# Dummy matmuls, transpose order and a copy's engine in the start-up of a two-layer SSM and GeGLU kernel

## The chip, the cores and the metric

The kernel runs on one core of a Trainium2 chip. The metric is the device time of one execution in microseconds (us).

## What is computed

Two layers, each a state-space block with a long convolution (A) followed by a gated feed-forward block (B), with shared weights, on 2048 rows of 576 features. The long convolution goes through a Fourier transform in the reference.

```python
def _A_ref(q, k, v, shift_k, ssm_k, ssm_D):
    ...                                   # k_shift: causal taps of k with shift_k (4 of them)
    kv = k_shift * v
    ...                                   # y = causal convolution of kv with ssm_k over 2048 rows
    y = y + kv * ssm_D[None, None, :]
    return q * y

def _B_ref(x, w_gate, w_up, w_down):
    return (_gelu(x @ w_gate) * (x @ w_up)) @ w_down

x = A_q
x = x + _A_ref(_layernorm(x, axis=-1), A_k, A_v, A_shift_k, A_ssm_k, A_ssm_D)
x = x + _B_ref(_layernorm(x, axis=-1), B_w_gate, B_w_up, B_w_down)
x = x + _A_ref(_layernorm(x, axis=-1), A_k, A_v, A_shift_k, A_ssm_k, A_ssm_D)
x = x + _B_ref(_layernorm(x, axis=-1), B_w_gate, B_w_up, B_w_down)
```

The features are 576, the feed-forward width 4608, the rows 2048; everything that comes in or goes out is bf16.

## The kernel before

The rows are cut into four blocks of 512, and each block into four row tiles of 128 (row `4p + i` of a block lies on partition `p`). The convolution is done block by block with a transform of 512 points written as matmuls: forward transform of the filter block and of `kv`, products on VectorE, inverse transform on TensorE. Block 0 needs only filter block 0, block 1 needs blocks 0 and 1, and so on.

The program has two stages.

**The start-up** (to about 45 us) does the convolution of block 0, the gate and the layernorm behind it, and the first gate and up matmuls. Its instructions are not written in a fixed order: `add(engine, cost, run, deps, ...)` enters a task with an estimated cost, and `Plan.order` simulates the engines with these costs. For each engine it takes, among the tasks that could start within 0.25 us of the earliest, the one with the highest rank plus priority (`prio`), where the rank is the longest chain of costs behind the task. A task that needs one of four PSUM banks (`bank=True`) gets one that is free, and a bank is free once the tasks in `frees` are over. The engines then run their instructions in this order, each waiting for its data.

In order of time the start-up holds, with the lines that matter here:

- dummy matmuls of `ones` by `ones` into bank 3 (L1139), 20 of them;
- four taps (L1197): a matmul broadcasts a row of `shift_k` over the partitions, ScalarE copies it (L1201). The last tap has dummy matmuls of its own behind it (`spare`, L1190);
- the shifted products: VectorE multiplies `k` by a tap (L1217), TensorE sums over the taps with identity matrices (L1226), VectorE multiplies by `v` (L1237);
- filter block 0 is transposed on TensorE (L1255, `turned_h0`), two groups of ten transposes. The 576 features are four pieces of 128 rows and one of 64. ScalarE copies each group (L1257), and VectorE adds `ssm_D` to one row (L1302);
- the forward transforms (L281 and L275), ScalarE's copies (L1293, L1319), VectorE's products (L316 to L320) and sums (L1347);
- the inverse transform for the four row tiles (L1361), each into a bank of its own;
- filter block 1 is transposed (L1275, `turned_h1`) into columns of these banks that the inverse leaves unused; VectorE copies the result, a small piece (L1277) and a large one (L1280), for each of two groups;
- dummy matmuls (`busy`, L1380), eight tasks of four, with priority -100;
- for each row tile: ScalarE's factor (L1408), VectorE's gate (L1417), ScalarE's square (L1436), GpSimd's root (L1445 and L1446), VectorE's norm (L1453), TensorE's transposes (L1467, and L1465 for a pair that is 64 columns wide), and a copy to `xnT`, on VectorE for row tiles 0 and 1 (L1472) and on ScalarE for 2 and 3 (L1475). The order of the tiles is 2, 0, 3, 1. ScalarE also keeps `y` for layer 1 (`keep`, L1428);
- the first halves of the first two gate and up blocks (`half_of`, L1008 with 256 columns), which need only row tiles 0 and 2. The second halves follow in the loop and need 1 and 3.

**The feed-forward loop** goes over units (layer, block) in three phases of the weights each. For each of 12 columns of a phase it does gate and up (L1008, TensorE), gelu (ScalarE) and a product (VectorE), then the down matmuls (L1601). Between these it fits in the convolution of the next blocks (L290, L301 and L343 on TensorE, products on VectorE). What goes in where is decided while the program is built, by a running estimate of the engines' times (`Pace`: `t.pe`, `t.dve`, `t.act`), which starts from what the start-up's plan leaves over. While block 1 is being made (`hurry`), a gelu takes one of two branches: with `t.act <= t.pe + 0.2` ScalarE copies the up half too and VectorE multiplies two bf16 tiles (L1572 to L1574); else VectorE multiplies straight out of PSUM (L1582, L1583).

Of the kernel before, what the change touches and what calls it, by code (L numbers as in the profile page):

```python
# [10 lines left out]
ACT = mybir.ActivationFunctionType  # L11
# [6 lines left out]
P = 128  # L18
# [4 lines left out]
HW = 288  # L23
# [48 lines left out]
class Plan:  # L72
# [8 lines left out]
    def add(self, eng, cost, run=None, deps=(), lat=0.0, bank=False, frees=(), ready=0.0, prio=0.0):  # L81
        task = Task(eng, cost, run, [d for d in deps if d is not None], lat, bank, list(frees), ready, prio)
        for b in task.frees:
            b.users += 1
        self.tasks.append(task)
        return task
# [607 lines left out]
def ssm_geglu_kernel(ctx, tc, A_q, A_k, A_v, A_shift_k, A_ssm_k, A_ssm_D, B_x, B_w_gate, B_w_up,  # L694
                     B_w_down, out):
    nc = tc.nc
    q2 = A_q[0]
    out2 = out[0]
    S, D = q2.shape
# [9 lines left out]
    NKC = D // HK  # L709
# [19 lines left out]
    def bank(n, name, shape=(P, 2, 512), dt=F32):  # L729
        return banks[n].tile(list(shape), dt, tag="pr", name=name)  # L730
# [358 lines left out]
    with tc.manual_schedule():  # L1089
# [3 lines left out]
        ND = D // P + 1  # L1093
        plan = Plan(4)
        add = plan.add
        with ExitStack() as es:
# [17 lines left out]
            for grid in (ident, below):  # L1114
                nc.gpsimd.memset(grid[:], 0.0)
            nc.sync.dma_start(out=sk1[SK:SK + 1, :, :].rearrange("p d j -> p (d j)"),
                              in_=A_shift_k.rearrange("d j -> (d j)").unsqueeze(0))
# [17 lines left out]
            warm = tmp.tile([P, 1], F32, name="warm")  # L1135
            nc.scalar.activation(out=warm[:], in_=conv.pis[:], func=ACT.Sin)
            ps = bank(3, "ps")
            for _ in range(20):
                nc.tensor.matmul(ps[:, 0, 0:P], lhsT=ones[:], rhs=ones[:], start=True, stop=True)  # L1139

            held = {}
# [1 line left out]
            def psum(key, task, shape=(P, 2, 512), dt=F32):  # L1143
                held[key] = bank(task.slot, "ps", shape, dt)
                return held[key]

            def chain(tasks):
                for a, b in zip(tasks, tasks[1:]):
                    b.deps.append(a)

            def later(make):

                box = []
                box.append(make(lambda f: (lambda: f(box[0]))))
                return box[0]
# [4 lines left out]
                out=jT[:, i, :, :], in0=colT[:], scalar=rowT[:, i:i + 1], in1=offs[:], op0=ALU.mult, op1=ALU.add), prio=50.0)  # L1160
# [25 lines left out]
            vneg = add("ACT", 0.9, vnegs, [vsin], prio=-20.0)  # L1186

            def spare(ps):
                for _ in range(2):
                    nc.tensor.matmul(ps[:, 1, 3 * P:4 * P], lhsT=ones[:], rhs=ones[:], start=True, stop=True)  # L1190


# [15 lines left out]
            for i0 in range(0, RT, 2):  # L1208
                accs = {i0: [], i0 + 1: []}
                first = {}  # L1210
                for j in range(conv.KS - 1, -1, -1):
# [9 lines left out]
                    for i in (i0, i0 + 1):  # L1221
# [7 lines left out]
                        a = later(lambda me: add("PE", 0.25, me(acc), [mults[-1]], bank=(j == conv.KS - 1), prio=20.0))  # L1229
# [5 lines left out]
                for i in (i0, i0 + 1):  # L1235
                    chain(accs[i])
                    kv0[i] = add("DVE", 0.74, lambda i=i: nc.vector.tensor_tensor(  # L1237
                        out=conv.halves(conv.vt_[0][:, i, :]), in0=held.pop(("kv", i))[:, :, 0:HW],
# [4 lines left out]
            hT, pairs1 = {}, []  # L1243
            hT0 = hp.tile([P, RT, D], BF16, tag="h", name="h")

            def turned_h0():
                outs = []
                hT[0] = lambda i: hT0[:, i, :]
                for g in range(RT // 2):
                    def fill_ps(task, g=g):  # L1250
                        pt = psum(("h", g), task, (P, 2, 1024), BF16)
                        for i in range(2):
                            for db in range(ND):
                                w = min(P, D - db * P)
                                nc.tensor.transpose(pt[:, i, db * P:db * P + w], hn[0][0:w, db, 2 * g + i:BS:RT], ident[0:w, 0:w])  # L1255
                    a = later(lambda me: add("PE", 1.05, me(fill_ps), bank=True, ready=HN_AT, prio=30.0))
                    outs.append(add("ACT", 1.12, lambda g=g: nc.scalar.copy(out=hT0[:, 2 * g:2 * g + 2, :], in_=held.pop(("h", g))[:, :, 0:D]),  # L1257
                                    [a], lat=0.1, frees=[a], prio=30.0))
                return outs

            def turned_h1(dep):


                W = D - P
                beside = lambda j: held["y", j].bitcast(BF16)
                hT[1] = conv.ht[1] = lambda i: pairs1[i // 2][:, i % 2, :]
                for g, j in ((0, 3), (1, 1)):
                    def fill_ps(g=g, j=j):
                        pairs1.append(conv.hrp.tile([P, 2, D], BF16, tag="hr", name="ht"))
                        for i in range(2):  # L1270
                            for db in range(ND):
                                w = min(P, D - db * P)
                                out = beside(j)[:, i, 2 * HW + (db - 1) * P:2 * HW + (db - 1) * P + w] if db else \
                                    beside(0)[:, g, 2 * HW + i * P:2 * HW + (i + 1) * P]
                                nc.tensor.transpose(out, hn[1][0:w, db, 2 * g + i:BS:RT], ident[0:w, 0:w])  # L1275
                    a = add("PE", 1.0, fill_ps, dep + [opened[0], opened[j], facs[j]], prio=-30.0)
                    add("DVE", 0.2, lambda g=g: nc.vector.tensor_copy(  # L1277
                        out=pairs1[g][:, :, 0:P], in_=beside(0)[:, g, 2 * HW:2 * HW + 2 * P].rearrange("p (i d) -> p i d", i=2)),
                        [a], frees=[opened[0]], prio=-10.0)
                    add("DVE", 0.6, lambda g=g, j=j: nc.vector.tensor_copy(  # L1280
                        out=pairs1[g][:, :, P:D], in_=beside(j)[:, :, 2 * HW:2 * HW + W]), [a], frees=[opened[j]], prio=-20.0 if g else -30.0)

            h0 = {}

# [24 lines left out]
            for m in KTS:  # L1309
                K0[m] = []  # L1310
                for s in range(2):
                    def fill_ps(task, m=m, s=s):
                        if s == 0:
# [3 lines left out]
                    a = later(lambda me: add("PE", 0.99, me(fill_ps), list(kv0.values()) + [tneg if m else tsin], bank=True,  # L1317
                                           prio=-4.0 * KTS.index(m)))
                    K0[m].append(add("ACT", 0.65, lambda m=m, s=s: nc.scalar.copy(  # L1319
                        out=kc[m][:, :, s * HW:(s + 1) * HW] if m == KTS[-1] else conv.halves(kc[m][:, s, :]),  # L1320
                        in_=held.pop(("k", m, s))[:, :, 0:HW]), [a], lat=0.1, frees=[a]))
# [34 lines left out]
            inv, opened = {}, {}  # L1356
# [6 lines left out]
            for i in (0, 2, 1, 3):  # L1363
# [5 lines left out]
                for kt, hs in ((0, (0, 1)), (1, (0, 1)), (3, (0,)), (3, (1,))):  # L1369
# [3 lines left out]
                                                      prio={(1, 0): -40.0, (0, 3): 10.0}.get((i, kt + hs[0]), 4.0 if i == 2 else 0.0))))  # L1373
# [4 lines left out]
            def busy():  # L1378
                for _ in range(4):
                    nc.tensor.matmul(held["y", 0][:, 1, 416:512], lhsT=ident[:], rhs=ident[:, 0:96], start=True, stop=True)  # L1380
            chain([add("PE", 0.22, busy, [inv[1], inv[3], opened[0]], frees=[opened[0]], prio=-100.0) for _ in range(8)])


            g0 = gvars[0]
# [19 lines left out]
            for j in (0, 2, 1, 3):  # L1404
# [33 lines left out]
                near = 10.0 if j in (0, 2) else 0.0  # L1438
                sq = add("ACT", 0.77, square, [gp], lat=0.05, prio=near if j else 0.0)

                def root(j=j):
# [2 lines left out]
                    ve = small.tile([P, 1], F32, tag="ve", name="ve")  # L1444
                    nc.gpsimd.tensor_scalar(out=ve[:], in0=v["ss"][:], scalar1=1.0 / D, scalar2=EPS, op0=ALU.mult, op1=ALU.add)  # L1445
                    nc.gpsimd.tensor_tensor(out=v["rstd"][:], in0=ve[:], in1=neghalf_t[:, 0:1], op=ALU.pow)  # L1446
                rt = add("POOL", 1.07, root, [sq], prio=near)

                def norm(j=j):
                    v = vs0[j]  # L1450
# [6 lines left out]
                def turn_xn(task, j=j):  # L1457
                    if 0 not in xnT_of:
                        xnT_of[0] = xtp.tile([P, NKC, CH], BF16, tag="xnT", name="xnT")
                    pt = psum(("xt", j), task, (P, 2, 1024), BF16)  # L1460
                    for b in range(NKC):
                        c0 = b * P if b < 5 else HK + (b - 5) * P
                        if b == 4:
                            for r0, c0 in ((0, 4 * P), (HK, 0)):
                                nc.tensor.transpose(pt[r0:r0 + HK, 0, 4 * P:5 * P], held["xn", j][:, c0:c0 + HK], ident[:])  # L1465
                            continue
                        nc.tensor.transpose(pt[:, b // 8, (b % 8) * P:(b % 8 + 1) * P], held["xn", j][:, c0:c0 + P], ident[:])  # L1467
                tx = later(lambda me: add("PE", 0.73, me(turn_xn), [no], bank=True))
                tok = slice(j * P, (j + 1) * P)
                view = lambda j=j: held["xt", j][:].rearrange("p a b -> p (a b)")[:, 0:NKC * P].rearrange("p (b q) -> p b q", q=P)  # L1470
                if j < 2:
                    c = add("DVE", 0.76, lambda tok=tok, view=view: nc.vector.tensor_copy(out=xnT_of[0][:, :, tok], in_=view()),  # L1472
                            [tx], frees=[tx])
                else:
                    c = add("ACT", 1.03, lambda tok=tok, view=view: nc.scalar.copy(out=xnT_of[0][:, :, tok], in_=view()),  # L1475
                            [tx], lat=0.1, frees=[tx])
                early_xn.append([c])


            turned_h1([loads[1]])  # L1480
            conv.nhr = 6
            conv.hr_free[0] = conv.hr_free[1] = NEVER
# [39 lines left out]
        for at, (wb, ph, ui, first, final) in enumerate(visits):  # L1522
# [33 lines left out]
            for fi in range(FP):  # L1556
                n, gi = divmod(wb * FP + fi, FG)
                w = wgu[n]
# [141 lines left out]
```

## Time and profile before

| | |
|---|---|
| three timed runs | 925.32, 927.99, 927.9 us; median 927.9 |
| profiled execution | 925.07 us, span 923.3 us |
| TensorE busy | 914.4 us (99%), 8101 matmuls |
| VectorE, ScalarE, GpSimd busy | 580.2, 326.0, 146.1 us |
| start-up, to 46.06 us: TensorE, VectorE, ScalarE busy | 44.31, 37.37, 33.10 us |
| largest group | L1008, gate and up, 5148 matmuls, 561.1 us |

The profile is of one execution. Times of the timeline count from the start of the span. A group's line gives the line of the code, the engine, the tile and what it is made from, and the shapes; what stands in brackets is the idle time of the engine just before and who ended it. A matmul's length includes its way through the array, so matmuls that follow each other overlap, and the distance of their starts tells the rate. The chain of waits is followed back from the last instruction to the first.

### The profile page before, as it was taken

To read this page: it belongs to the slowest core of one execution; us is meant where nothing else is said; L and a number is where in the kernel's file an instruction comes from. 1 tells how busy PE (TensorE), PEld (TensorE's weight loads), DVE (VectorE), ACT (ScalarE), POOL (GpSimd) and SP (SyncE) were. 2 spreads that over 40 slices of the span, in tenths; PEclk is the share of its full clock that TensorE was granted. 3 is DMA by queue.
4 is the path that set the end of the run, shared out by engine and by line. 5 is a ranking of instruction groups with operands and counts; after the bars stand their busy time and mean duration, and the time that the engine had idled before them with its cause. 6 is when DMAs were issued, how large, how long until landed. Compare 5 with 4: busy or idle time off the path is not lost.

```text
span 923.3 us, 19170 instructions
## 1 busy us (share of the span) xinstructions
PE 914.4 (99%) x8101; PEld 528.7 (57%) x8101; DVE 580.2 (63%) x1106; ACT 326.0 (35%) x594; POOL 146.1 (16%) x314
## 2 busy tenths in 40 slices
PE   9999999999999999999999999999999999999998
PEld 7746556565564665655645646546546556556555
DVE  8785885777898898768888874552333334432332
ACT  7674435533215145252123233451221224321211
POOL 5323102312114013230112101220000002100000
PEclk9999999999999999999999999999999999999999
DMA  9999996429617801992943820790820820787620
GB/s 239 278 265 257 241 251 115 127 67 252 190 48 177 229 1 28 250 250 48 254 137 94 162 67 29 131 190 13 155 78 1 152 81 14 138 209 169 140 65 27
DMA packets 125307, 129.69 MB, mean 140 GB/s; under 512 B 39714, under 2 KB 117411, under 8 KB 125220
## 3 DMA queue, kind: packets, MB, share of 16 engines
q1 hardware_dynamic: 116018, 92.92, 47.3%
q0 software_dynamic: 9056, 34.95, 11.6%
q8 instruction: 63, 1.03, 0.5%
q10 hardware_dynamic: 146, 0.59, 0.2%
q14 instruction: 24, 0.20, 0.1%
HBM read 108.09 MB, written 11.80 MB: 130 GB/s over the span
## 4 chain that ended last, share of the span: by engine, by line
PE 94%; DVE 3%; DMA 1%; ACT 0%; issue 0%; POOL 0%; SPq 0%; ACTq 0%; DVEq 0%
PE gu L1008 61%; PE dn L1601 28%; PE ps L281 1%; PE cps L290 1%; PE cps L343 1%; DMA hn<-in_A_ssm_k_dram 1%; DVE kc L602 1%; PE cps L301 0%; PE ps L1008 0%; PE ps L1226 0%; DVE ab L308 0%; DVE x_c L1417 0%; DVE cd L308 0%; ACT eo L303 0%; DMA xnT<-xn 0%
## 5 line engine op out<-in xcount | busy, mean ns | idle before, releaser
L1008 PE MATMUL gu<-xnT,wgu 64*128 64x512 bf16 x5148 | 561.1, 376 | 2.3 <-DVE x_c L1643 1.5
L1008 PEld LDWEIGHTS <-wgu 64*128 64x128 bf16 x5220 | 255.0, 94 | 304.6 <-issue 9.9
L1582 ACT ACTIVATE ga<-gu 128x512 f32<-128x512 f32 x256 | 152.8, 597 | 471.4 <-PE gu L1008 465.2
L1583 DVE TENSOR_TENSOR hT<-ga,gu 128x512 bf16<-128x512 f32 x256 | 175.6, 686 | 204.8 <-ACT ga L1582 203.3
L1601 PE MATMUL dn<-wd,hT 128*128 128x288 bf16 x2304 | 294.1, 286 | 0.0
L1601 PEld LDWEIGHTS <-hT 128*128 128x128 bf16 x2304 | 223.5, 98 | 65.3 <-issue 9.3
L840 POOL TENSOR_SCALAR means<-s 128x1 f32<-128x1 f32 x28 | 12.7, 453 | 236.7 <-DVE x_c L1637 205.3
L1645 DVE TENSOR_TENSOR x_c<-x_c,dn 128x576 f32<-128x576 f32 x32 | 24.1, 753 | 30.9 <-PE dn L1601 30.8
L1643 DVE SCALAR_TENSOR_TENSOR x_c<-dn,means,x_c 128x576 f32<-128x576 f32 x28 | 22.7, 815 | 26.8 <-PE dn L1601 26.7
L856 POOL TENSOR_TENSOR rstd<-ve,neghalf_t 128x1 f32<-128x1 f32 x56 | 35.2, 628 | 4.7
L320 DVE TENSOR_TENSOR prod<-prod 128x576 bf16<-128x576 bf16 x72 | 33.0, 458 | 2.5
L1572 ACT ACTIVATE ga<-gu 128x512 bf16<-128x512 f32 x30 | 17.9, 597 | 44.0 <-PE gu L1008 43.0
L303 ACT ACTIVATE eo<-cps 128x576 f32<-128x576 f32 x32 | 20.4, 650 | 25.0 <-DVE ab L308 9.8
L418 POOL DMA_DIRECT2D kr<-Kd x24 | 13.3, 553 | 87.2 <-DVE prod L319 86.0
L1624 DVE TENSOR_TENSOR xn<-x_c,dn 128x576 bf16<-128x576 f32 x15 | 11.3, 753 | 23.9 <-PE dn L1601 23.9
L422 POOL DMA_DIRECT2D hr<-Hd x36 | 19.5, 543 | 40.9 <-DVE prod L319 38.7
L1574 DVE TENSOR_TENSOR hT<-ga 128x512 bf16<-128x512 bf16 x31 | 13.1, 421 | 20.4 <-ACT ga L1573 20.4
L602 DVE TENSOR_TENSOR kc<-ab,cd 128x288 bf16<-128x288 f32 x64 | 25.6, 451 | 0.0
L840 POOL TENSOR_SCALAR nm<-s 128x1 f32<-128x1 f32 x28 | 8.7, 312 | 99.8 <-DVE x_c L892 99.8
L848 ACT ACTIVATE junk<-x_c,nm 128x576 bf16<-128x576 f32 x28 | 21.5, 767 | 4.9 <-POOL nm L840 4.9
L882 ACT ACTIVATE yh<-y,rstd 128x576 f32<-128x576 bf16 x28 | 21.4, 768 | 2.3 <-POOL rstd L856 2.3
L855 POOL TENSOR_SCALAR ve<-ss 128x1 f32<-128x1 f32 x56 | 15.2, 271 | 43.3 <-ACT junk L848 43.2
(180 smaller groups left out, 612.1 us busy)
## 6 DMA issues: line engine op xcount, KB each, us to landing
wgu<-in_B_w_gate_dram SPq DMA_DIRECT2D x45, 576.0 KB, 6.1
wd<-in_B_w_down_dram SPq DMA_DIRECT2D x30, 864.0 KB, 8.0
wgu<-in_B_w_up_dram SPq DMA_DIRECT2D x45, 512.0 KB, 8.3
hr<-Hd POOLq DMA_DIRECT2D x36, 288.0 KB, 7.3
kr<-Kd POOLq DMA_DIRECT2D x24, 288.0 KB, 5.9
Kd<-kc POOLq DMA_DIRECT2D x12, 288.0 KB, 6.7
k<-in_A_k_dram POOLq DMA_DIRECT2D x3, 1008.0 KB, 11.2
wgu<-in_B_w_up_dram SPq DMA_DIRECT2D x45, 64.0 KB, 8.4
```

The source lines that it names most:

```text
L320: nc.vector.tensor_tensor(out=dst[:, cols], in0=pr[:, 0, cols], in1=pr[:, 1, cols], op=ALU.subtract if part == 0 else ALU.add)
L602: nc.vector.tensor_tensor(out=into[k][:, plane, cols], in0=a, in1=b, op=op)
L840: nc.gpsimd.tensor_scalar(out=v["nm"][:], in0=v["s"][:], scalar1=-1.0 / D, scalar2=None, op0=ALU.mult)
L848: nc.scalar.activation(out=junk[:], in_=get_x(), func=ACT.Square, bias=v["nm"][:, 0:1], accum_out=v["ss"][:])
L856: nc.gpsimd.tensor_tensor(out=v["rstd"][:], in0=ve[:], in1=neghalf_t[:, 0:1], op=ALU.pow)
L882: nc.scalar.activation(out=g["yh"][:], in_=conv.y[c][:, j, :], func=ACT.Identity, scale=g["rstd"][:, 0:1], bias=1.0)
L1008: nc.tensor.matmul(cols(pair[:, s, :]), lhsT=w[r0:r0 + HK, k, gi * P:(gi + 1) * P], rhs=cols(xnT[r0:r0 + HK, blk_of[k], :]), start=(k == 0 ...
L1582: nc.scalar.activation(out=ga[:], in_=pair[:, 0, :], func=ACT.Gelu_apprx_tanh)
L1583: nc.vector.tensor_tensor(out=hT[:, fi, :], in0=ga[:], in1=pair[:, 1, :], op=ALU.mult)
L1601: nc.tensor.matmul(acc[:, h, 0:HW], lhsT=hT[:, fi, j * P:(j + 1) * P], rhs=wd[2 * wb + fi // WT][:, fi % WT, h * HW:(h + 1) * HW], start=( ...
L1643: nc.vector.scalar_tensor_tensor(out=xh, in0=acc[:, :, 0:HW], scalar=m_[:, 0:1], in1=xh, op0=op, op1=ALU.add)
L1645: nc.vector.tensor_tensor(out=xh, in0=xh, in1=acc[:, :, 0:HW], op=ALU.add)
```

## The change

- The dummy matmuls at the start become 24 instead of 20, and those behind the last tap (`spare`) five instead of two.
- The transposes of both filter blocks go over the feature pieces first and the two row tiles second, so that a group does its eight transposes of 128 rows and then its two of 64 rows.
- The large copies of filter block 1 go from VectorE to ScalarE.
- The dummy tasks behind the inverse become four instead of eight, and their estimated cost 0.18 instead of 0.22.
- In the transposes of `xn` the pair that is 64 columns wide comes last.
- The copy of row tile 3 to `xnT` goes from ScalarE to VectorE.
- The root's estimated cost becomes 0.92 instead of 1.07.

```diff
-            for _ in range(20):
+            for _ in range(24):
                 nc.tensor.matmul(ps[:, 0, 0:P], lhsT=ones[:], rhs=ones[:], start=True, stop=True)
...
             def spare(ps):
-                for _ in range(2):
+                for _ in range(5):
...
                         pt = psum(("h", g), task, (P, 2, 1024), BF16)
-                        for i in range(2):
-                            for db in range(ND):
-                                w = min(P, D - db * P)
+                        for db in range(ND):
+                            w = min(P, D - db * P)
+                            for i in range(2):
...
                         pairs1.append(conv.hrp.tile([P, 2, D], BF16, tag="hr", name="ht"))
-                        for i in range(2):
-                            for db in range(ND):
-                                w = min(P, D - db * P)
+                        for db in range(ND):
+                            w = min(P, D - db * P)
+                            for i in range(2):
...
-                    add("DVE", 0.6, lambda g=g, j=j: nc.vector.tensor_copy(
-                        out=pairs1[g][:, :, P:D], in_=beside(j)[:, :, 2 * HW:2 * HW + W]), [a], frees=[opened[j]], prio=-20.0 if g else -30.0)
+                    add("ACT", 0.84, lambda g=g, j=j: nc.scalar.copy(
+                        out=pairs1[g][:, :, P:D], in_=beside(j)[:, :, 2 * HW:2 * HW + W]), [a], lat=0.1, frees=[opened[j]], prio=-20.0 if g else -30.0)
...
-            chain([add("PE", 0.22, busy, [inv[1], inv[3], opened[0]], frees=[opened[0]], prio=-100.0) for _ in range(8)])
+            chain([add("PE", 0.18, busy, [inv[1], inv[3], opened[0]], frees=[opened[0]], prio=-100.0) for _ in range(4)])
...
-                rt = add("POOL", 1.07, root, [sq], prio=near)
+                rt = add("POOL", 0.92, root, [sq], prio=near)
...
-                    for b in range(NKC):
+                    for b in sorted(range(NKC), key=lambda b: b == 4):
...
-                if j < 2:
+                if j != 2:
                     c = add("DVE", 0.76, lambda tok=tok, view=view: nc.vector.tensor_copy(out=xnT_of[0][:, :, tok], in_=view()),
```

## The prediction

> **What bounds the kernel now.** The page's first part gives TensorE 914.4 of 923.3 us, so I looked for where it is not busy, or busy with nothing useful. All edits lie ahead of the feed-forward loop, which starts at about 43 us, so I read the chain of waits over that stretch first:
>
> ```profile
> 1.61 5.41 DMA hn<-in_A_ssm_k_dram
> 7.07 1.72 PE ps L1255 x16
> ...
> 36.92 0.48 DVE ht L1277 x2
> 37.40 0.49 DVE xn L1453
> 37.89 0.54 DVE ht L1280
> ...
> 40.93 2.07 PE ps L1008 x36
> 43.00 0.45 PE ps L1380 x8
> 43.45 1.09 PE ps L1008 x18
> ```
>
> Three places count. A filter load releases the transposes at 7.07. From 28 to 38 us the chain runs on VectorE, two filter copies among its links. And eight dummy matmuls (L1380) stand between the first halves of gate and up and the second. Next, TensorE's timeline (start, length, tile, idle time):
>
> ```profile
> 1.08 2.31 PE L1139 MATMUL ps<-ones 128*128 128x128 bf16 x20 [1.08 <-DVE ones L1111]
> ...
> 5.93 0.65 PE L1226 MATMUL ps<-kvt,below 128*128 128x288 bf16 x4 [0.16 <-ACT skc L1201]
> 6.42 0.39 PE L1255 MATMUL ps<-ident,hn 128*128 128x128 bf16 x4
> 7.07 1.72 PE L1255 MATMUL ps<-ident,hn 64*128 64x64 bf16 x16 [0.26 <-DMA hn<-in_A_ssm_k_dram]
> ```
>
> The dummies stand 0.107 us apart, the transposes of 6.42, as wide, 0.056: TensorE runs at half rate first and at full rate by 6.4. Then VectorE's timeline behind the inverse:
>
> ```profile
> 36.35 0.57 DVE L1453 TENSOR_SCALAR xn<-x_c,nm,rstd 128x576 bf16<-128x576 f32 x1
> ...
> 37.80 0.62 DVE L1280 COPY ht<-ps 128x896 bf16<-128x896 bf16 x1
> 38.34 0.57 DVE L1453 TENSOR_SCALAR xn<-x_c,nm,rstd 128x576 bf16<-128x576 f32 x1
> 38.82 0.62 DVE L1280 COPY ht<-ps 128x896 bf16<-128x896 bf16 x1
> 39.36 0.57 DVE L1453 TENSOR_SCALAR xn<-x_c,nm,rstd 128x576 bf16<-128x576 f32 x1
> ```
>
> VectorE has no gap here; each copy holds the next norm back by 0.54. In the loop itself TensorE waits four times for more than half a microsecond, 3.63 us in all:
>
> ```profile
> 164.18 0.61 PE L1008 MATMUL gu<-xnT,wgu 64*128 64x512 bf16 x4 [0.68 <-DMA xnT<-xn]
> 194.28 0.40 PE L301 MATMUL cps<-ht,T 128*128 128x288 bf16 x2 [0.83 <-ACT eo L303]
> 240.83 0.61 PE L1008 MATMUL gu<-xnT,wgu 64*128 64x512 bf16 x4 [1.49 <-DVE x_c L1643]
> 413.04 0.41 PE L301 MATMUL cps<-v,T 128*128 128x288 bf16 x2 [0.63 <-ACT eo L303]
> ```
>
> **Dummies at the start.** Four more at 0.107 are 0.43 us. The first tap matmul writes the dummies' bank and starts at 3.45, right after their end (1.08 + 2.31 = 3.39); it moves to 3.88. The first tap copy on ScalarE moves from 4.16 to 4.59, the first product on VectorE from 4.83 to 5.26, and the first sums (L1226), which wait for the third copy, from 5.93 to 6.36. The three added spare matmuls at 0.076 end by 6.3, within that wait. They delay the last tap copy, which waits for them, by 0.23 more, and behind it on ScalarE the sine table and the filter copies; ScalarE idles 0.34 before the latter (7.83), and VectorE gets to their user (L1302) only at 9.4. So nothing; 0.3 us if that cover is too thin.
>
> **Transposes of filter block 0.** Read one by one, a transpose starts 0.056 after the last, but 0.15 after a change between 128 and 64 rows. After the change the eight 128-row ones follow the sums (6.36 + 4 x 0.1225 = 6.85) up to 7.3, and the 64-row piece has landed by then (7.02). Two at 7.39, the second group's eight from 7.60, its two at 8.22, and the next sums at 8.43 instead of 8.72: minus 0.29. What is late next is VectorE: six products from 5.26 end at 9.36, L1302 at 9.83, and the first product with v starts at 9.87 instead of 10.16. That still gives 0.28. Ends: nothing, if VectorE is a little later than I make it, and 0.7, if the taps did not move (the sums at 8.02). From 13.6 to 34.2 TensorE runs without a gap, so the 0.28 carries through.
>
> **Filter block 1.** Its transposes (34.17 to 36.19) lose four changes, some 0.4 us, worth nothing: only dummies follow. The two copies leave VectorE. The four norms, at 36.35, 37.32, 38.34 and 39.36, are then paced by GpSimd's roots, which end at 36.0, 37.0, 37.7 and 38.6; 0.28 earlier, with two short copies between, I get 36.07, 36.84, 37.6 and 38.36. The last one ends at 38.93. Its transposes took 0.74; with the 64-column pair last, one change less, I take 0.65, ends 0.56 and 0.74. They follow the third row's, 39.07 to 39.72. The copy for row 0, behind the last norm on VectorE, ends at 39.59. So the first half starts at about 39.75 instead of 40.87: 1.12 earlier, 0.84 of it here. On ScalarE a copy of 896 elements has no row; between 0.65 (576) and 1.11 (1152) I take 0.87, near the 0.99 of 1024. Its priority puts both behind the four squares: 37.11 to 37.98, then row 2's copy to 39.0, then the second to 39.75. The first frees the bank of the third row's transposes (wanted at 38.3), the second possibly that of the first half: cover 0.3 and nothing, so up to 0.3 dearer. The four results kept for layer 1 are queued behind, to 42.75; the first gelu needs ScalarE at 42.9. Row 3's copy on VectorE (0.75, L1472) ends at 40.3 and row 1's at 41.0; the second halves want them at 41.8.
>
> **Dummies behind the inverse.** Of 32, 24 lie in waits for norms (36.19 and 37.72) and eight on the path, 0.45. The 16 left fit into the first of those waits and the next, so minus 0.45; if one task of four still fell behind the first halves, minus 0.22.
>
> **Sum.** 0.28 + 0.84 + 0.45 = 1.57 us, ends 0.5 and 2.2. The profiled execution took 925.07 (span 923.27 and 1.80 outside), so its like comes to 923.5. The loop gets another start: the planner's surplus of ScalarE work goes, worked through its costs in the code, from 0.58 to 1.37, and the first block's gelu then takes the branch of L1582 instead of L1572. Later choices may shift; of the 3.63 us of waits some may go and others come. I take nothing for it, ends minus 1.5 and plus 1.5.
>
> **The rivals.** *The start of the clock.* The profiled execution and one timed run are at 925.07 and 925.32, the other two at 927.9 and 927.99. Half rate for 5.5 us more of TensorE work on the path costs 2.75 us, and from 5.93 to 13.6 that work is nearly unbroken; so the gap fits a full rate that came late in two of four. No trace of a 927.9 run is here. The change makes the first dense stretch 2.6 us long instead of 2.1 and puts work before the wait at 5.93. If that makes the early start regular, the median joins the lower group: 925.2 - 1.57 = 923.6, my forecast, 0.50. If the groups stay as they are, or have another cause, it is 927.9 - 1.57 = 926.3, 0.20. The Trainium skill, "TensorE: Matmul & The Clock Gate", Part 1, says that the clock opens after one sufficiently busy window of about 3.4 us that runs free of the program's start; the trace agrees with one opening between 3.2 and 6.4, and shows nothing of its spread. By that rule the two groups are two places of the window.
>
> *The clock falls again, with half the dummies gone.* From 33.9 to 39.75 only transposes and 16 dummies run. At half rate the work from there costs as much again; with the 5.2 us from 40.87 to 46.06 doubled it is 2.6 to 5.2 dearer: 926 to 929. Against it: from 38.48 to 40.87 the trace has transposes alone and no fall, 0.056 apart throughout. 0.04. The same page, Part 4, says that transposes do not count as activity to the clock; this trace shows no such thing.
>
> *The loop's rhythm*, the side of slower. At 164.18 TensorE waits 0.68 for block 1's last row, which hangs on a chain from 155.32 (transposes, VectorE, GpSimd, a transposing DMA) of 8.9 us, so far covered by matmuls of L1601 and two of L1008. The changed order of the first blocks can make that row later; up to 8.1 us more lies bare. From 4.4 us later on, the gain of 1.57 is gone and 0.3% lost: 928 by the profile; at 6 us 929.5, and about 931 beside the median. For it: the order is decided by estimated times. Against it: VectorE starts its share of block 1 earlier too. 0.16.
>
> *The start-up does not do as summed* (a bank or a dummy task in the way): 925 to 928, no change, 0.10.
>
> **The numbers.** A measurement tells 0.3%, 2.8 us, from no change: faster is under 925.1, slower above 930.7. Of the first case nearly all is faster, of the others a little: 0.53. Slower is most of the rhythm's case and a little of the others: 0.15. The rest is 0.32. Range 922.0 to 930.5, out of which lie some 5% below and 14% above; the likeliest case alone has 922.4 to 925.0.
>
> **What would show it.** Right: 24 dummies, first tap at 3.9; no wait between the transposes at 7; L1226 at 8.4; norms about 0.75 us apart with no L1280 among them; first half of gate and up at 39.7 to 39.9; no L1380 behind it; the second at 41.8. Wrong: first half later than 40.5, a TensorE wait in the loop of over 2 us, or spacing of 0.107 after 34 us.

## The result, and the profile after

The kernel after takes 923.72 us (median of ten runs, 923.68 to 924.16). The kernel before takes 925.33 us (ten runs, 924.73 to 927.99, the three shown ahead of the change among them). The ratio of the two is estimated at 0.9978, with a 95% interval of 0.9969 to 0.9988; the medians alone, 1.6 us apart, give 0.9983. So the gain is 0.2%. Of the three runs shown ahead of the change two belong to an upper group near 927.9, called dear below, so their median is well above that of the ten. The profiled execution of after took 923.70 us, its span is 921.9; before, 925.07 and 923.3.

The chain of waits of after, over the start-up (start, length, what):

```profile
6.36 0.65 PE ps L1226 x4
7.01 1.38 PE ps L1255 x20
...
37.87 0.78 POOL rstd L1446
...
38.67 0.59 DVE xn L1453
```

No DMA stands in front of the transposes of L1255 any more, and they end at 8.39 instead of 8.79. No filter copy is left in the chain behind the inverse; GpSimd's roots (L1446) stand there in its place. TensorE's timeline shows both:

```profile
3.88 2.20 PE L1197 MATMUL ps<-sk,ones 97*128 97x288 bf16 x8
...
6.85 1.54 PE L1255 MATMUL ps<-ident,hn 128*128 128x128 bf16 x20
8.32 0.91 PE L1226 MATMUL ps<-kvt,below 128*128 128x288 bf16 x6
...
40.04 3.12 PE L1008 MATMUL ps<-xnT,wgu 64*128 64x256 bf16 x54
```

The 54 matmuls of the last line are the first half of gate and up (36) and the second (18) in one piece, without the dummies of L1380 between them. The first half starts 0.83 earlier than before (40.87). The second, which begins with the 37th of these matmuls, starts at 42.02 instead of 43.38: 1.36 earlier. The last two of VectorE's norms (the first two start at 35.95 and 36.64), and their roots on GpSimd:

```profile
37.65 0.58 DVE L1453 TENSOR_SCALAR xn<-x_c,nm,rstd 128x576 bf16<-128x576 f32 x1 [0.25 <-POOL rstd L1446]
38.67 0.58 DVE L1453 TENSOR_SCALAR xn<-x_c,nm,rstd 128x576 bf16<-128x576 f32 x1 [0.44 <-POOL rstd L1446]
```

```profile
36.77 0.85 POOL L1446 TENSOR_TENSOR rstd<-ve,neghalf_t 128x1 f32<-128x1 f32 x1
...
37.87 0.77 POOL L1446 TENSOR_TENSOR rstd<-ve,neghalf_t 128x1 f32<-128x1 f32 x1
```

The same two roots in before:

```profile
37.17 0.76 POOL L1446 TENSOR_TENSOR rstd<-ve,neghalf_t 128x1 f32<-128x1 f32 x1
...
38.03 0.55 POOL L1446 TENSOR_TENSOR rstd<-ve,neghalf_t 128x1 f32<-128x1 f32 x1
```

Both norms now wait for their roots; before, VectorE had no gap there. In the loop the four waits stand where they stood, and are as long (0.68, 0.83, 1.49 and 0.63 before):

```profile
162.82 0.82 PE L1008 MATMUL gu<-xnT,wgu 64*128 64x512 bf16 x6 [0.70 <-DMA xnT<-xn]
192.91 0.41 PE L301 MATMUL cps<-ht,T 128*128 128x288 bf16 x2 [0.84 <-ACT eo L303]
239.49 0.61 PE L1008 MATMUL gu<-xnT,wgu 64*128 64x512 bf16 x4 [1.50 <-DVE x_c L1643]
411.70 0.41 PE L301 MATMUL cps<-v,T 128*128 128x288 bf16 x2 [0.63 <-ACT eo L303]
```

They come 1.34 to 1.37 us earlier, and the span is 1.34 shorter (921.93 instead of 923.27): what was won by 43 us is still there at the end.

### The profile page after: what moved, and what is told of

Its sections match the earlier page's. It is cut to its first block, busy times and chain, and to the rows that moved or that the text cites. A ratio compares the mean times of both kernels' runs of the same rounds, so it can differ in the third digit from the quotient of the medians.

```text
span 921.9 us, 19151 instructions
## 1 busy us (share of the span) xinstructions
PE 913.0 (99%) x8092; PEld 528.0 (57%) x8092; DVE 579.8 (63%) x1105; ACT 326.6 (35%) x595; POOL 144.8 (16%) x314
## 4 chain that ended last, share of the span: by engine, by line
PE 95%; DVE 2%; ACT 1%; POOL 1%; issue 0%; DMA 0%; ACTq 0%; DVEq 0%; SPq 0%
PE gu L1008 61%; PE dn L1601 28%; PE ps L281 1%; PE cps L290 1%; PE cps L343 1%; DVE kc L602 1%; PE cps L301 0%; PE ps L1226 0%; PE ps L1008 0%; PE ps L1361 0%; DVE ab L308 0%; DVE cd L308 0%; POOL rstd L1446 0%; PE ps L1139 0%; ACT eo L303 0%
## 5 line engine op out<-in xcount | busy, mean ns | idle before, releaser
L1582 ACT ACTIVATE ga<-gu 128x512 f32<-128x512 f32 x256 | 152.9, 597 | 471.4 <-PE gu L1008 464.0
```

The costliest lines, as they stand in the source:

```text
L1582: nc.scalar.activation(out=ga[:], in_=pair[:, 0, :], func=ACT.Gelu_apprx_tanh)
```

## The experiments

The times are medians; in brackets the lowest and the highest run. A ratio is to the runs of before beside the variant, with its 95% interval. Variants of after are to be held against its 923.72. They ran beside different sets of runs of before; the lowest run of each set is at 924.72 to 924.74, so the sets can be compared.

### The start of the clock

**Before, two more profiles.** No edit: two more executions of the kernel before, to see what a dear one looks like.

> The kernel before once more, for a second profile of it. 13 of 33 and 10 of 35 of its runs beside the other experiments were at 927.5 to 928, the rest near 925. Theory (the clock opens late in the dear executions): if the profiled execution takes about 927.7, matmuls of equal width stand at half rate well past 6.4 us, to about 12 us, TensorE's transposes of filter block 0 and the forward transform behind it take twice as long, and the first half of gate and up starts near 43.5 instead of 40.87, with the loop unchanged. Rival (something later, a wait in the loop): the first half at 40.9 and a new TensorE wait of about 2.6 us in the loop. If the execution is near 925 it shows nothing but the repeat.

> The same kernel once more, for another chance of an execution at 927.7; the same expectations.

One took 924.94, the other 927.90 us. TensorE's timeline of the dear one:

```profile
5.93 1.12 PE L1226 MATMUL ps<-kvt,below 128*128 128x288 bf16 x4
6.85 2.97 PE L1255 MATMUL ps<-ident,hn 128*128 128x128 bf16 x20
...
12.60 1.02 PE L1182 MATMUL ps<-ident,T 128*128 128x128 bf16 x8
13.46 1.15 PE L281 MATMUL ps<-h,T 128*128 128x288 bf16 x8
```

Up to 5.93 it runs as the cheap ones. Then the sums stand 0.23 apart instead of 0.1225, the eight matmuls of L1182 0.107 instead of 0.056, and only L281 at 13.46 runs at full rate: its eight take 1.15, as before (1.14). L281 started at 10.65 in the profile before, so the half rate cost 2.81 us; the executions differ by 2.83. In the trace's record of the granted clock the rise to full rate is at 13.44 us here, at 4.24 in the profile before and at 5.69 in the other execution, of 924.94 us. (The record begins with that rise. What stands ahead of it is told by the distances of the matmuls alone.) The loop has nothing to do with it: TensorE's waits in it are 0.70, 0.84, 1.49 and 0.63, as ever.

So the two groups of before are an early and a late start of the clock. Which of them comes changes from one execution of the same program to the next: of 33 runs of before beside four of the variants 13 were at 927.5 to 927.9, of 35 beside four others 10 at 927.6 to 928.0. Three of each lie at 926.0 to 926.1; of those there is no trace.

**Before with the dummies of after.**

```diff
-            for _ in range(20):
+            for _ in range(24):
...
-                for _ in range(2):
+                for _ in range(5):
```

> The kernel before with only the dummies at the start changed, 24 and 5 instead of 20 and 2. In 33 runs beside the first experiments the kernel before had 17 runs from 924.7 to 925.5, 3 near 926.0 and 13 from 927.5 to 927.9. Theory (the dummies make the full clock start early enough in every execution): the sums behind filter block 0 start at 8.8 instead of 8.72, all runs lie between 924.8 and 925.6, none above 926.5; median about 925.0. Rival (the high runs have another cause): 3 to 5 of 10 runs above 927 again.

925.29 us (925.15 to 925.53, eleven runs), ratio to before 0.9994 [0.9985, 1.0002]. None of the runs is dear, while before beside it went from 924.73 to 927.98. The dummies alone take the dear executions away; lowest run against lowest run they cost 0.4 us (the sums are at 8.99 in the profile, not 8.72).

**After with the dummies of before.**

```diff
-            for _ in range(24):
+            for _ in range(20):
...
-                for _ in range(5):
+                for _ in range(2):
```

> The changed kernel with the dummies at the start put back to 20 and 2; all else as changed. Theory (the dummies cost the path nothing but make the full clock start regular): in an execution whose clock opens early the first tap is back at 3.45 us, the sums behind filter block 0 start at about 8.0 instead of 8.3, so such a run takes 923.4 to 923.7; but of the runs some 2 in 10 stand 2 to 3 us above the lowest, as in the kernel before (924.73 to 927.99), where the changed kernel lies within 0.5 us (923.68 to 924.16). Rival (the spread has nothing to do with the dummies): all runs within 0.6 us. Second rival (the dummies do cost the path): median lower than 923.4 with no high run.

923.50 us, nine runs: seven at 923.28 to 923.88, two at 924.66 and 925.10. Ratio 0.9976 [0.9964, 0.9987].

> The variant with 20 dummies in front and two spare ones once more. It had two of nine runs above 924.5, the one with 20 and five none of twelve. Theory (the three spare matmuls behind the last tap make the early clock regular): again two to four of about eleven runs lie above 924.5, the others at 923.2 to 923.5. Rival (those two were chance, and the change in the order of the transposes already made the start regular): all runs at 923.2 to 923.9.

The same once more: eight of twelve runs at 923.26 to 923.47, four at 925.00 to 925.18 (median 923.37). So six of 21 runs are dear without the added dummies, and the others 0.3 to 0.4 us cheaper than after. The rival, that the order of the transposes makes the start regular, is out. The dear ones lie 1.3 to 1.9 us above the cheap ones here, against 2.8 in before; no dear execution of this variant was profiled, so why it is less isn't shown.

**After with 20 in front and the five spare ones.**

```diff
-            for _ in range(24):
+            for _ in range(20):
```

> The kernel after with 20 dummies in front instead of 24, the five spare ones kept. Taps at 3.45 instead of 3.88, as in the variant with 20 and 2 (its fast runs at 923.3 to 923.5, its slow ones to 925.1). If the wait behind the last tap, filled by the spare ones, is what lets the clock stay half: 923.3 to 923.5 in all runs, 0.3 under after, profile's sums at 8.1. If it is the length of the first dense stretch: the spread of 1.8 us returns, with some runs at 924.5 to 925.1 and a median about that of after.

923.37 us (923.25 to 923.86, twelve runs), ratio to before 0.9974 [0.9965, 0.9983]. Cheap, and none dear. TensorE's timeline:

```profile
5.47 0.46 PE L1190 MATMUL ps<-ones 128*128 128x128 bf16 x5
5.93 0.65 PE L1226 MATMUL ps<-kvt,below 128*128 128x288 bf16 x4
...
8.16 0.91 PE L1226 MATMUL ps<-kvt,below 128*128 128x288 bf16 x6
```

The taps are back at 3.45, and the five spare matmuls fill the wait ahead of the sums at 5.93 (0.16 with two, in before's profile). Filling that wait is enough; the four more dummies in front are not needed. (At the rate of the variant with 20 and two, 6 of 21, twelve runs without a dear one would come by chance about once in 55 times. Four more in front without the three spare ones were not run.) This version beats both kernels: by 0.35 us against after (ten of its twelve runs are under after's lowest), and by 2 us against before.

**After with hardly any dummies.**

```diff
-            for _ in range(24):
+            for _ in range(8):
...
-                for _ in range(5):
+                for _ in range(2):
```

> The changed kernel with 8 dummies at the start and 2 behind the last tap instead of 24 and 5. Theory: TensorE starts its dense work late, the full clock opens later, in many runs behind 7 us, and from 5.9 to 13 us each microsecond at half rate costs half a microsecond: median 924.5 to 926, runs spread over 2 us or more; in the profile matmuls of 288 columns 0.24 us apart instead of 0.1225 somewhere behind 6 us. Rival (the clock does not depend on the dummies): taps start at 2.3 to 2.5, all runs within 0.6 us at or below 923.4.

924.97 us (924.49 to 925.51, eleven runs), ratio 0.9987 [0.9977, 0.9997]. All runs lie above after's median, by 0.8 to 1.8 us. Its timeline:

```profile
3.54 2.20 PE L1197 MATMUL ps<-sk,ones 97*128 97x288 bf16 x8 [1.42 <-DMA sk<-in_A_shift_k_dram]
...
6.01 1.12 PE L1226 MATMUL ps<-kvt,below 128*128 128x288 bf16 x4
```

In this execution the taps start at 3.54, when their data has landed. 20 dummies end shortly before that (3.39); the four added ones, which end at 3.82 in after, only delay the taps. The eight taps take as long as ever, 2.20, though the clock rises only at 10.1 here; the sums behind run at half rate, and the next ones, at 8.32 in after, start at 9.34.

### The order of the transposes

After with the transposes of both filter blocks in the order of before (row tile first, then feature piece); the edit is the same at both places.

```diff
-                        for db in range(ND):
-                            w = min(P, D - db * P)
-                            for i in range(2):
+                        for i in range(2):
+                            for db in range(ND):
+                                w = min(P, D - db * P)
```

> The changed kernel with the transposes of both filter blocks in the old order (row tile by row tile, four changes between 128 and 64 rows in a group instead of two). Theory: only filter block 0 is on the path; the sums behind it start at 8.7 to 8.8 instead of 8.32, all behind them moves by 0.4 to 0.5, and the median is 924.1 to 924.2. Rival (block 1's transposes count as well): twice that, first half of gate and up at 40.9, median 924.6. Rival (VectorE sets the pace there, the order gives nothing): 923.7.

924.01 us (923.98 to 924.28, twelve runs), ratio 0.9979 [0.9970, 0.9988]: the order is worth 0.3 us. In its profile the sums start at 8.81 (after: 8.32) and the first half at 40.34 (40.04), so 0.49 is lost at the place, and 0.19 of it is made good before 40 us. The last norm is at 38.66, no later than in after, since the third and fourth root on GpSimd took only 0.68 and 0.57 us here, against 0.85 and 0.77.

### The copies of filter block 1

**Back on VectorE,** and row tile 3's copy back on ScalarE.

```diff
-                    add("ACT", 0.84, lambda g=g, j=j: nc.scalar.copy(
...
+                    add("DVE", 0.6, lambda g=g, j=j: nc.vector.tensor_copy(
...
-                if j != 2:
+                if j < 2:
```

> The changed kernel with filter block 1's large copies back on VectorE and row tile 3's copy back on ScalarE. Theory by the trace after the change (GpSimd's roots pace the norms, so only part of what the copies cost is won): last norm at about 39.0 to 39.1 instead of 38.67, first half of gate and up 0.4 us later than 40.04, median 924.1. Rival, as the prediction had it (0.84 us from the copies): first half at 40.9, median 924.5.

924.02 us (923.98 to 924.26, eleven runs), ratio 0.9977 [0.9968, 0.9987]: 0.3 us, a third of the 0.84 forecast. That is the time expected, but it does not come about as expected, by a later last norm. VectorE's timeline shows that (a copy stands between the last two norms, and they are where after has them, 37.65 and 38.67), and TensorE's what costs the 0.3:

```profile
38.14 0.62 DVE L1280 COPY ht<-ps 128x896 bf16<-128x896 bf16 x1
38.68 0.57 DVE L1453 TENSOR_SCALAR xn<-x_c,nm,rstd 128x576 bf16<-128x576 f32 x1
```

```profile
38.91 0.61 PE L1467 MATMUL ps<-ident,xn 128*128 128x128 bf16 x8 [0.29 <-ACT xnT L1475]
...
40.36 3.12 PE L1008 MATMUL ps<-xnT,wgu 64*128 64x256 bf16 x54
```

Here the copy does not hold the norms back; the roots do (the fourth ends at 38.63). Row tile 3's transposes wait for the PSUM bank of row tile 2, until ScalarE has copied it, and row tile 1's then stand behind them without a gap. This is not the order of before, though: there both large copies stood between the norms (37.80 and 38.82), and here the second one runs behind the last norm (39.83). The program orders by its estimated costs, and this variant keeps the root's new one, 0.92. No run takes that cost back alone, so what it brings by itself isn't shown.

**The roots made shorter.** If the roots are the new pace, a part of them taken from GpSimd should bring the norms forward. Each root's first instruction (L1445) goes to VectorE.

```diff
-                    nc.gpsimd.tensor_scalar(out=ve[:], in0=v["ss"][:], scalar1=1.0 / D, scalar2=EPS, op0=ALU.mult, op1=ALU.add)
...
+                    nc.vector.tensor_scalar(out=ve[:], in0=v["ss"][:], scalar1=1.0 / D, scalar2=EPS, op0=ALU.mult, op1=ALU.add)
...
-                rt = add("POOL", 0.92, root, [sq], prio=near)
+                rt = add("DVE", 0.15, root, [sq], prio=near)
+                rt = add("POOL", 0.65, power, [rt], prio=near)
```

> The changed kernel with the first of the root's two small GpSimd instructions (scale and epsilon, L1445) moved to VectorE, for the four row tiles of the start-up. Theory (GpSimd's roots pace the norms after the change, 0.25 and 0.44 us of waits on VectorE): the last norm starts 0.45 to 0.7 earlier than 38.67, first half of gate and up at 39.4 to 39.6 instead of 40.04, median 923.1 to 923.3. Rival (the transposes and VectorE are next at once): first half 0.2 earlier, 923.5. Rival (the added VectorE instructions wait in its queue ahead of the gates): later than 40.04, 924 or more.

923.83 us (923.82 to 924.13, eleven runs), ratio 0.9981 [0.9973, 0.9990]: nothing gained. The last norm does start earlier, at 38.54 instead of 38.67, but TensorE has another wait:

```profile
38.00 0.61 PE L1471 MATMUL ps<-ident,xn 128*128 128x128 bf16 x8 [0.40 <-ACT ht L1280]
```

The second row tile's transposes (at 37.47 in after) wait until ScalarE has copied filter block 1 out of a bank; from there TensorE runs without a gap to the first half at 40.18, 0.14 later than in after. In after the same transposes started while that copy ran (36.98 to 37.86), so they had another bank there: the new costs have changed the choice of banks as well. Shorter roots alone were not tested; what the variant shows is that a bank can take their place as the limit.

### The dummies behind the inverse

**Eight tasks again,** with the old cost.

```diff
-            chain([add("PE", 0.18, busy, ..., prio=-100.0) for _ in range(4)])
+            chain([add("PE", 0.22, busy, ..., prio=-100.0) for _ in range(8)])
```

> The changed kernel with eight dummy tasks behind the inverse at the old cost of 0.22 instead of four at 0.18. By the program's order eight of the 32 matmuls stand between the first and the second halves of gate and up again. Theory: first halves where they are after the change (40.0 to 40.1), second halves 0.45 later (42.55 instead of 42.1), median 924.1 to 924.2. Rival (the time is made up in the loop, which has waits of its own): 923.7.

924.68 us (924.64 to 924.79, eleven runs), ratio 0.9986 [0.9977, 0.9995]: 0.96 us dearer than after, nearly twice what eight dummies between the halves cost. The rest lies ahead of the transposes:

```profile
37.55 0.50 PE L1380 MATMUL ps<-ident 128*128 128x96 bf16 x8
...
38.72 0.34 PE L1380 MATMUL ps<-ident 128*128 128x96 bf16 x4
...
42.61 0.51 PE L1380 MATMUL ps<-ident 128*128 128x96 bf16 x8
```

Eight dummies at 37.55 and four at 38.72 push the transposes to where the first half starts at 40.54 instead of 40.04 (0.50, of which 0.09 comes from further in front: the first norm is at 36.04 instead of 35.95). The second half, behind the other eight, starts at 43.05 instead of 42.02, 0.53 more.

**None at all.** The line that adds them is left out.

> The changed kernel without any dummy matmul behind the inverse. From 33.8 to 40 us TensorE then has transposes alone. Theory (transposes keep the clock, and the 16 dummies lie in a wait): spacing stays 0.056 per 128 columns, first half at 40.04, median 923.6 to 923.8. Rival (transposes do not count as activity and the clock falls): matmuls of 256 columns 0.21 us apart instead of 0.11 behind 40 us, median 926 or more.

923.87 us, ratio 0.9982 [0.9974, 0.9991]; eight of twelve runs at 923.69 to 923.94, as after, and four at 924.85 to 925.07. The profiled execution is one of the four (924.90). Its timeline (the lines of the code are one lower here), and the table of stretches (their bounds and length, the busy time of TensorE, its loads, VectorE, ScalarE and GpSimd, with the instructions, then the granted clock, the DMA share and GB/s):

```profile
38.29 0.99 PE L1466 MATMUL ps<-ident,xn 128*128 128x128 bf16 x8
...
40.67 3.54 PE L1008 MATMUL ps<-xnT,wgu 64*128 64x256 bf16 x52
```

```profile
34.80:38.30 3.50, 2.29 (x29) 1.61 (x29) 3.12 (x11) 3.50 (x8) 3.15 (x8) 1.00 0.96 327
38.40:41.70 3.30, 3.30 (x30) 2.39 (x30) 2.67 (x4) 3.30 (x5) 0.23 (x1) 0.50 1.12 229
```

The granted clock falls to half from 38.37 to 41.79 us, 3.41 us in all, and comes back to 1.00. Eight transposes take 0.99 from start to end in it, 0.62 in after. In the 3.4 us ahead of the fall TensorE did nothing but transposes, with a wait of 1.06 among them. The 16 dummies that after keeps cost no time, and with them no run of after showed this.

## Why the prediction was right, and where its steps were off

**The start of the clock**, the likeliest case, is what happened: the expensive group of before was a full rate that came late, and after has no such runs. Its price, 2.75 us, the text took from the gap between the timed runs; the dear execution has 2.81. The time comes out at 923.72 against 923.6. The forecast put 925.2 under it as the level of the lower group, which 17 of the 33 runs beside the first experiments have (924.7 to 925.5). But counted from the ten runs' median, 925.33, the change brings 1.6 us, below the 2.8 us that the text calls a measurable gain; only from the three runs' median, 927.9, is it more. The reason for the regular start was half right: work in the wait at 5.93 is enough for it, the longer first stretch is not needed. The Trainium skill, "TensorE: Matmul & The Clock Gate", Part 1, says that the window of about 3.4 us runs free of the program, so that the opening comes at another place in each run. The runs agree, with openings at 4.24, 5.69 and 13.44 us in three executions of one kernel and a fall that lasted 3.41. Counted back from 13.44 in steps of 3.41, two windows of the dear execution failed to open the clock, 3.2 to 6.6 and 6.6 to 10.0. The first holds the wait ahead of 5.93, and the eight taps too; the second holds 2.9 us of transposes. That these are the reasons is argued from their place. For the wait the variants with five spare matmuls support it; what the taps count for, and the second window, no run tests.

**Dummies at the start.** As summed: taps at 3.88, first sums at 6.36, no DMA wait ahead of the transposes. The text had them at nothing beyond what the front term contains; the variant with 20 and five shows that this 0.43 of delay costs 0.35 at the end, and is needless.

**Transposes of filter block 0.** Forecast 8.43 for the sums and a gain of 0.28 behind VectorE; measured 8.32 and 0.40 (the start of the matmuls of L1226 at 11.63 moved to 11.23, that of L1275 at 34.17 to 33.77). The term was too small by 0.12: the twenty transposes take 1.47 from start to start of the next work, not 1.58, and VectorE follows, L1237 at 9.76 instead of the 9.87 forecast.

**Filter block 1** is the step that was mis-sized: 0.84 forecast, 0.43 in the profile (0.83 at the first half less the 0.40 from the front), 0.3 when the copies are put back. The norms were forecast at 36.07, 36.84, 37.6 and 38.36; they came at 35.95, 36.64, 37.65 and 38.67. The first half came at 40.04, not at 39.7 to 39.9. The text named the roots as the next pace but took over their old distances, shifted by 0.28, and read the end of the third as 37.7, where its row in before (37.17, 0.76 long) gives 37.93. In after the third and the fourth root took 0.85 and 0.77 instead of 0.76 and 0.55, and the fourth ended at 38.65, later than the 38.6 before. Why the same instruction takes longer isn't shown. What the copies on ScalarE bring, by the variant without them, is a PSUM bank for row tile 3's transposes that is free earlier; the sum had banks only as a possible cost. The other 0.11 of the 0.43 is what the edits bring together that this variant keeps (the root's cost, the order in the transposes of `xn`, fewer dummies); the last row tile's transposes alone became 0.10 shorter, 0.73 from their first to the first half (39.31 to 40.04) instead of 0.83 (40.04 to 40.87). The copy of 896 elements on ScalarE, which had no row, took 0.88 and 0.91, against 0.87 estimated.

**Dummies behind the inverse.** 0.45 forecast, 0.53 in the profile (1.36 at the second half less 0.83 at the first): about right for this change. Put back into after they cost 0.96, since some of them then no longer lie in waits: the cover named in the text is thin.

**The sum** of the parts in the profile is 0.40 + 0.43 + 0.53 = 1.36, and 1.34 at the end of the span. Forecast was 1.57. That the time is met within 0.1 us is in part luck: the copies' term was too large by 0.41, the two others were too small by 0.12 and 0.08, and the base, 925.2, was one choice within a group that reaches from 924.7 to 925.5. Undone one at a time the three parts even make 0.3 + 0.3 + 0.96 = 1.56, with two of them far from their forecasts.

**The rhythm of the loop** did not change, as taken: four waits of the same lengths, though the first gelu took the other branch (L1582), as the text had it.

**The clock falls again.** In after it does not, so the low chance was borne out, but the argument for it was wrong. The transposes alone without a fall, from 38.48 to 40.87, last 2.4 us, less than the 3.41 for which the clock fell; they could not have shown one. Without dummies the fall is there, by the times, in a third of the runs, at 1.2 us, less than the 2.6 to 5.2 forecast, as it lasted only 3.41 us. The same page, Part 4, says that the transpose mode does not count as busy in the same way. With no other matmuls the trace agrees (2.29 us of transposes in 3.5, then a granted clock of 0.50), against what the prediction said of it. The rival, that the wait of 1.06 did it, does not fit: in after TensorE waits 1.50 us ahead of 239.49, in the 3.41 us from 236.35 it is busy for 1.91 with matmuls that are not transposes, and the granted clock stays at 1.00.

## What to carry to other kernels

Where the times of a kernel fall into two groups, look for the start of the clock: compare the distance of equal matmuls in a dear and a cheap execution, and fill the waits between the first matmuls before adding work ahead of them: a dummy that delays the first real matmul is paid for, and one in a wait is not. Dummies in a stretch of transposes could be halved here, but not left out, and only those that push real work cost time. When an engine is relieved, do not shift the next one's old times: work out the next one's own pace and the PSUM banks that its results wait for.

## What the runs showed of the hardware that was not expected

- The taps (L1197: 97 rows, 288 columns) take 0.255 us each whether the clock is at half or full rate: eight take 2.20 with the clock up at 4.24 us and at 10.1 us. So it costs nothing if the clock opens late within them: among the profiled executions of after and its variants with 24 and five dummies it opened between 4.17 and 6.34, and the runs of each of these variants lie within 0.5 us, but for the one without dummies behind the inverse.
- The fall of the clock behind the inverse lasted 3.41 us in the profiled execution, and the runs show it, by their times, only in some executions of the same program, with the same order of instructions.
- GpSimd's power of one element per partition (L1446) took 0.55 to 0.85 us in before and after, with the same shape and operands.
